# A convolution and attention mix: all of x loaded as rows, four buffers for VectorE's probabilities, GpSimd placed by VectorE, and 95 pairs of score tiles for VectorE

## The chip, the cores and the metric

The kernel runs on one core of a Trainium2 chip. The metric is device time in microseconds, the median of several runs; lower is better. A run takes a little longer than the span that its profile shows, from the first instruction to the last.

## The reference

x, k and v are 2048 tokens of 640 numbers in bfloat16. Two results are mixed by a gate of each token, `g = sigmoid(sum(x * gate_w))`.

```python
k_shift = sum over t of k_pad[:, t:t + S, :] * shift_k[:, ks - 1 - t]      # 4 taps along the tokens
kv = k_shift * v
y = causal convolution of kv with ssm_k along the tokens (by FFT) + kv * ssm_D
a = x * y
q = (x @ wq) as 32 heads of 20;  k = x @ wk;  v = x @ wv                  # one k and v for all heads
p = softmax((q . k) / sqrt(20));  b = (p . v) @ wo
out = g * a + (1 - g) * b
```

The convolution is done by matrices of cosines and sines (spectra of kv and ssm_k, a product, an inverse). The largest part is the softmax: 32 heads x 2048 x 2048 exponentials.

## The kernel before

**Attention.** The heads and token blocks make 32 groups `G` (four heads, 512 query tokens), each with 16 blocks `j` of 128 keys and four rows `r` (one for each head): 32 x 16 x 4 = 2048 score tiles of 128 x 512. A score is one matmul on 32 rows of TensorE (`score`, L1074), four rows side by side. ScalarE takes the exponential of three tiles in one call (`ETA`) and of two in the next (`ETB`), out of PSUM banks 0 to 4 (L1106). `PVmm` (L1146) multiplies the probabilities by v into bank 6, on 32 columns of TensorE for each row.

A table `DVE_J` gives for each group the key blocks of which two rows go to VectorE instead, a "pair": `DEXP` copies two scores out of banks 5 and 7 (L1135, `dW`) and evaluates a polynomial in three instructions of 128 x 1024 (L1138, L1139, L1141) into the one buffer `ETd`. Its PV, two matmuls with `vneg`, floats: it is put between the others when the pair is ready, and the last PV of the group waits for all pairs of the group.

**Beside it.** Between the scores TensorE does the shift of k (`kc`, L1325), the spectra (L1383) of five chunks of 128 channels, the inverse (L1449), the q projection of the next token block (L993), and the output projection (L1479); where it has nothing, it runs fillers on zeros (L1529). GpSimd multiplies the spectra (`mac`, L1416: `Pp`, then `AB`) and norms the attention's output (L1216). VectorE copies every result out of PSUM.

**Prologue.** Before the first exponential x must be there with its channels on the partitions (`xT`). Two of its four blocks of 512 tokens come by a DMA that transposes, issued by SP; the two others are loaded as rows (`xn`) and transposed on TensorE (L906), copied out by ScalarE (L631) and VectorE (L630). Then follow k, v and the gate's sum in one product (`kvn`, L942), the largest squared length of a key (`ksq`, `ksum`, `kmcol`, a broadcast on TensorE, `kmaxr`, `kroot`, `mcol`), which goes into k's row 21 as a bound for the softmax, the first q projection with its lengths (`sq`, `cr`, and a DMA of 8 KB into `qT`'s row 20, the "crow"), and `kT`, k for four rows. Eight sine and cosine tables of 128 x 513 are made by VectorE and ScalarE (L815 to L828). The two row blocks of x that came by the transposing DMA are loaded again as rows in the main part (`load_x`), for the gate and the product with x.

**What sets the order.** No order is written by hand. Every operation is recorded with what it reads and writes, a cost and a priority; `Scheduler` then places them one by one on five in-order engines, scores and exponentials first, the rest where the costs leave room, and emits each engine's list with semaphore waits. An instruction that waits holds up all that follow on its engine, in a list that was made by estimated costs.

## Time and profile before

| | before |
|---|---|
| median of 3 runs | 881.03 us (880.82 to 882.23) |
| the profiled execution's own time | 881.59 us |
| its span | 879.8 us |
| granted TensorE clock, mean | 0.999 |
| score tiles on VectorE, in pairs | 93 pairs |
| exponential calls on ScalarE | 745 |

The span is counted from the first instruction to the last; times of rows are from its start. A row of the view by time gives start, length, engine, line, operation, output and input, count, and in brackets how long the engine stood idle before it and what ended that. The chain of work that ended last is followed back from the last instruction, at each step to what released it. A group's row gives its busy time, the mean of one in ns, and the idle time ahead of it. In a table of stretches each engine's busy time stands with its count, and the last three columns are the granted clock, the DMA engines' busy share and GB/s.

### The profile page before, as it was taken

How to read it: one execution, taken by the hardware profiler on the slowest of the kernel's cores; microseconds unless marked ns; L12 is line 12 of the kernel's file. 1: busy time of each engine (PE TensorE's matmuls, PEld its weight loads, DVE VectorE, ACT ScalarE, POOL GpSimd, SP SyncE). 2: the span in 40 equal slices, each digit the busy share in tenths (PEclk: the TensorE clock that was granted, in tenths of full speed). 3: DMA queues.
4: the chain of work that ended last, by engine and by line, in shares of the span. 5: the costliest groups of instructions: out<-in, count | busy, mean ns of one | idle time of the engine just before them, and what ended most of it. 6: DMA issues, size and time to landing. Idle time of an engine off the chain costs nothing.

```text
span 879.8 us, 17975 instructions
## 1 busy us (share of the span) xinstructions
PE 852.8 (97%) x7783; PEld 345.5 (39%) x7804; DVE 683.1 (78%) x890; ACT 858.3 (98%) x770; POOL 434.3 (49%) x342
## 2 busy tenths in 40 slices
PE   7999999999999999999999999999999999999997
PEld 3335324442344334344334233444344444334333
DVE  6775887688878888887869886884878857878785
ACT  6999999999999999999999999999999999999995
POOL 2952005997064548734439823458764558510000
PEclk9999999999999999999999999999999999999999
DMA  8920310002000000100000111000000000302110
GB/s 160 222 80 20 57 30 21 13 9 43 20 20 20 14 9 19 45 19 20 13 17 11 44 38 39 20 10 11 20 20 19 14 13 2 102 22 74 51 36 32
DMA packets 55780, 31.98 MB, mean 36 GB/s; under 512 B 38547, under 2 KB 51732, under 8 KB 55700
## 3 DMA queue, kind: packets, MB, share of 16 engines
q1 hardware_dynamic: 53562, 29.79, 13.0%
q10 hardware_dynamic: 2138, 1.04, 0.5%
q8 instruction: 61, 1.00, 0.5%
q14 instruction: 19, 0.16, 0.1%
HBM read 17.85 MB, written 6.02 MB: 27 GB/s over the span
## 4 chain that ended last, share of the span: by engine, by line
ACT 84%; PE 12%; DMA 2%; DVE 1%; issue 0%; SPq 0%; DVEq 0%
ACT ETA L1106 51%; ACT ETB L1106 34%; PE ps L1074 4%; PE ps L1383 3%; PE ps L1146 2%; DMA xT<-in_A_q_dram 1%; PE ps L993 1%; PE ps L1529 1%; DMA qT<-cr 1%; PE ps L1325 0%; PE ps L1264 0%; DVE qT L1004 0%; PE ps L1015 0%; PE ps L1387 0%; DVE outsb L1288 0%; PE ps L1273 0%
## 5 line engine op out<-in xcount | busy, mean ns | idle before, releaser
L1106 ACT ACTIVATE ETA<-ps 128x1536 bf16<-128x1536 f32 (+1 forms) x373 | 582.7, 1562 | 1.5 <-PE ps L1074 1.1
L1106 ACT ACTIVATE ETB<-ps 128x1024 bf16<-128x1024 f32 x372 | 425.4, 1144 | 0.0
L1074 PE MATMUL ps<-qT,kT 32*128 32x512 bf16 x2048 | 302.1, 384 | 13.4 <-ACT ETA L1106 7.2
L1416 POOL TENSOR_TENSOR Pp<-X,K 128x512 f32<-128x512 bf16 x120 | 174.6, 1474 | 211.0 <-DVE K L1404 207.1
L1135 DVE TENSOR_SCALAR dW<-ps 128x512 f32<-128x512 f32 x186 | 127.5, 686 | 80.8 <-PE ps L1074 79.6
L1074 PEld LDWEIGHTS ps<-qT,kT 32*128 32x128 bf16 x2048 | 74.2, 91 | 243.6 <-ACT ETB L1106 118.5
L1146 PE MATMUL ps<-ETA,vaug 128*32 128x512 bf16 x1118 | 151.2, 385 | 0.0
L1146 PE MATMUL ps<-ETB,vaug 128*32 128x512 bf16 x744 | 148.8, 385 | 0.3 <-ACT ETA L1106 0.3
L1141 DVE SCALAR_TENSOR_TENSOR ETd<-dX,dW 128x1024 int16<-128x1024 f32 x93 | 126.1, 1356 | 13.4 <-PE ps L1146 13.3
L1138 DVE SCALAR_TENSOR_TENSOR dX<-dW 128x1024 f32<-128x1024 uint16 x93 | 129.8, 1395 | 1.1
L1139 DVE SCALAR_TENSOR_TENSOR dX<-dX,dW 128x1024 f32<-128x1024 f32 x93 | 125.4, 1348 | 0.4
L1416 POOL TENSOR_TENSOR AB<-Pp 128x256 bf16<-128x256 f32 x80 | 94.7, 1184 | 4.8
L1216 POOL TENSOR_TENSOR oTn<-acc,rbc 128x512 bf16<-128x512 f32 x24 | 38.1, 1588 | 90.6 <-DMA rbc<-scr_d 90.5
L1449 PE MATMUL ps<-AB,Tcos 128*128 128x256 bf16 x320 | 77.1, 275 | 0.0
L1529 PE MATMUL ps<-Tcos,zeros 128*32 128x512 bf16 x876 | 72.9, 385 | 0.0
L1416 POOL TENSOR_TENSOR Pp<-Pp 128x512 f32<-128x512 f32 x40 | 68.7, 1718 | 2.8
L1449 PE MATMUL ps<-AB,Tsin 128*128 128x256 bf16 x280 | 68.6, 275 | 0.0
L1216 POOL TENSOR_TENSOR oT<-acc,rbc 128x512 bf16<-128x512 f32 x7 | 12.1, 1732 | 94.1 <-DMA rbc<-scr_d 94.1
L1383 PE MATMUL ps<-ssm_kT,Tcos 128*128 128x256 bf16 x320 | 55.7, 276 | 0.0
L1383 PE MATMUL ps<-ssm_kT,Tsin 128*128 128x256 bf16 x320 | 51.1, 275 | 0.0
L1383 PE MATMUL ps<-kv,Tsin 128*128 128x256 bf16 x320 | 50.2, 274 | 0.0
L1383 PE MATMUL ps<-kv,Tcos 128*128 128x256 bf16 x320 | 49.0, 275 | 0.0
(140 smaller groups left out, 790.0 us busy)
## 6 DMA issues: line engine op xcount, KB each, us to landing
rbc<-scr_d SPq DMA_DIRECT2D x31, 256.0 KB
scr_o<-oTn SPq DMA_DIRECT2D x24, 128.0 KB, 1.9
kv<-in_A_v_dram SPq DMA_DIRECT2D x4, 640.0 KB
out_dram<-outsb SPq DMA_DIRECT2D x14, 160.0 KB, 2.8
xn<-in_A_q_dram SPq DMA_DIRECT2D x3, 640.0 KB
oTp<-scr_o SPq DMA_DIRECT2D x12, 160.0 KB, 2.9
wog<-in_B_wo_dram SPq DMA_DIRECT2D x4, 200.0 KB
wo<-in_B_wo_dram SPq DMA_DIRECT2D x4, 200.0 KB
```

The lines of the kernel that those rows point to most:

```text
L1074: return e.matmul(self.bank(bk), T["kT4"][32 * r:32 * r + 32, 128 * j:128 * j + 128], T[f"qT{G // 8 % 2}"][32 * r:32 * r + 32, G % 8, :], ...
L1106: op("act", lambda e: e.activation(et(n)[:, 0:w], self.ps[:, lo:lo + w], ACT.Exp, scale=SCALE), [("ps", base[n % 2] + k) for k in range(le ...
L1135: self.evac(gr, "dve", lambda e, bk, h=h: e.tensor_scalar(W[:, 512 * h:512 * h + 512], self.bank(bk), SCALE * LOG2E * 128.0, 128.0 * (127 ...
L1138: V(lambda e: e.scalar_tensor_tensor(X[:, :], w, DP, w, ALU.add, ALU.mult), [kW], ["dX"], c_ps(1024), **k)
L1139: V(lambda e: e.scalar_tensor_tensor(X[:, :], X[:, :], DQ, w, ALU.add, ALU.mult), [kW], ["dX"], c_ps(1024), **k)
L1141: V(lambda e: e.scalar_tensor_tensor(T["ETd"][:, :].bitcast(dt.int16), X[:, :], DA, W[:, :], ALU.mult, ALU.add), [kW, "dX"], ["ETd"], c_ps ...
L1146: return op("pe", lambda e: e.matmul(self.bank(6)[32 * r:32 * r + 32, :], T[va][:, j, :], src, start=(j == 0), stop=(j == NSC - 1), tile_p ...
L1216: self.pool(lambda e: e.tensor_tensor(out, T["acc"][:, :], T["rbc"][:, :], ALU.mult), ["acc", "rbc"], [key], c_pool(512), prio=p, port=Tru ...
L1383: self.mm(gr, lambda e, bk, lhs=lhs, rhs=rhs, comp=comp, n=n: e.matmul(self.bank(bk, 256, 256 * comp), lhs, rhs, start=(n == 0), stop=(n = ...
L1416: f = lambda e: e.tensor_tensor(out, a, b, alu)
L1449: self.mm(gr, lambda e, bk, lhs=lhs, fc=fc, comp=comp, h=h: e.matmul(self.bank(bk, 256, 256 * h), lhs, AB[:, fc, :, comp, :], start=(fc == ...
L1529: sch.filler = [[lambda e, r=r, st=st: e.matmul(self.bank(6)[32 * r:32 * r + 32, :], self.T["zeros"][:, 0:32], self.T["Tcos"][:, 0, 0:512] ...
```

## The change

It has six parts.

1. **x.** All four blocks of x are loaded as rows, first on SP's queue, and transposed on TensorE (80 transposes instead of 40). A channel of x goes to partition and chunk in another order (`dc:D:NDC`), and the rows of wk, wv, wq and gate_w with it, so that each partition reads one piece. `load_x` is gone.
2. **The rest of the prologue.** The first q projection is of one group instead of two; v's and the gate's copies out of the work tile go to GpSimd; `mcol` is a TENSOR_SCALAR; the first kT block is copied in two parts (128 and 384 columns), and the scores wait for the part that they read (`kkey`). The tables are made from column 128 c on; the part to its left is the transposed part of the other tables, made by TensorE after the first exponential. Many tiles share memory with others.
3. **VectorE's pairs.** `ETd` has four buffers (`NED`). Two floating pairs on different rows are put together (`join`), or a pair goes into a PV of two rows that leaves its rows free (`hole`).
4. **GpSimd.** `pool_may` lets the scheduler place a GpSimd instruction only while VectorE is in one that isn't marked `port`, or after it has waited long; and the instruction then waits for the VectorE instruction before that one.
5. **95 pairs** in another table `DVE_J`, in which a group has up to five.
6. `ssm_kT` has one buffer instead of two; the output's buffers lie over `qT0`.

```diff
+YOUNG = 4.0
+WAITN = 0.5
+HOLD = 0.1
+WAITP = 3.0
 PVB = 2
 NET = 3
+NED = 4
+NXK = 3
...
+        if e == "pool" and self.main_started and not self.pool_may(t):
+            return None
...
+    def pool_may(self, t):
+        d = self.order["dve"]
+        if not d or not HOLD:
+            return True
+        x = d[-1]
+        if not x.port and x.end > t + HOLD:
+            return True
+        w = [o.ready + (WAITP if o.name != "onorm" else WAITN) for o in self.cand["pool"] if o.ready <= t]
+        return bool(w) and t > min(w)
...
+                    self.join(f, t)
+                    return f
+        elif m.hole:
+            for f in self.floats:
+                if f.ready <= t and f.cols <= m.hole:
+                    self.floats.remove(f)
+                    self.float_left = list(f.tail)
+                    for x in f.tail:
+                        x.cost = 0.003
                     return f
...
+    def join(self, f, t):
+
+        for g in self.floats:
+            if g.ready <= t and not (g.cols & f.cols):
+                self.floats.remove(g)
+                self.float_left[-1].cost = 0.003
+                self.float_left += [g] + list(g.tail)
+                return
...
+        if e == "pool" and self.main_started and HOLD:
+            d = self.order["dve"]
+            if len(d) > 1 and d[-1].end > t and not d[-1].port:
+                op.deps.add(d[-2])
...
-DVE_J = [(6,), (), (2, 9, 14), (4, 10), (2, 9), (1, 2, 8, 12), (2, 7, 12), (2, 6, 10, 14), (3, 9), (1, 5, 12), (1, 7, 11), (2, 6, 10, 14), (2, 7, 12), (1, 4, 8, 12), (2, 5, 10), (1, 8), (2, 6, 10, 14), (3, 4, 13), (1, 4, 8, 12), (1, 9), (2, 10, 12), (3, 9), (2, 7, 12), (2, 5, 10, 14), (3, 6, 12), (1, 3, 9, 13), (12,), (3, 8, 13), (1, 6, 11), (3, 11, 12), (1, 5, 9, 13), (1, 5, 8, 12)]
+DVE_J = [(), (3, 11), (1, 6, 11), (2, 11), (2, 6, 10, 14), (3, 4, 9, 12), (3, 9), (1, 6, 11), (2, 8, 13), (1, 2, 7, 12), (2, 6, 10, 14), (3, 9), (1, 7, 10), (8,), (1, 4, 7, 10, 13), (3, 9), (1, 4, 8, 13), (2, 4, 8, 12), (1, 6, 11, 14), (6,), (3, 5, 8, 10), (1, 4, 8, 12), (8,), (1, 4, 7, 10, 13), (1, 4, 7, 10, 13), (1, 6, 11), (4,), (1, 4, 7, 10, 14), (2, 5, 8, 12, 14), (4, 11), (5,), (2, 9)]
...
-        for b in range(NB - 2):
-            o = T["xT"][:, :, 512 * b:512 * b + 512]
-            i = aps["A_q"][0][512 * b:512 * b + 512, :]
-            xl = self.g.add("sp", lambda e, o=o, i=i: e.dma_start_transpose(o, i), (), [("xT", b)], 0.1, kind="d",
-                            nbytes=655360, prio=-8 + b, lat=3.3)
-            xl.iss = 3.8
...
+        for b in range(NB):
+            xl = self.dma(T["xn"][:, 4 * b:4 * b + 4, :], x[:, 4 * b:4 * b + 4, :], writes=[("xn", b)], nbytes=655360,
+                          prio=-9 + b, lat=3.0)
...
+        wq = aps["B_wq"].rearrange("(p dc) n -> p dc n", dc=NDC)
+        self.dma(T["wqst"][:, :, 0:80], wq[:, :, 0:80], writes=[("wqst", 0)], eng="act", prio=-98.65,
+                 lat=4.5)
...
+            lo = 128 * c
+            n = W - lo
...
+            sins.append(self.op("act", lambda e, c=c, t=t, lo=lo: e.activation(
+                T["Tcs"][:, :, c, lo:W], t[:, :, lo:W], ACT.Sin, bias=T["pi_col"][:, :], scale=-2.0 * math.pi / L),
+                [("tprod", c), "pi_col"], [("Tsin", c), ("Tcos", c)], c_act(2 * n), **k))
...
+        for name in ("Tsin", "Tcos"):
+            gr = self.group("tabT", 12.0, banks=(7,))
+            for c in range(1, H):
+                for d in range(c):
+                    o = self.mm(gr, lambda e, bk, name=name, c=c, d=d: e.transpose(
+                        self.bank_bf(bk, 128, 64 * c * (c - 1) + 128 * d), T[name][:, d, 128 * c:128 * c + 128],
+                        T["ident"][:, :]), [(name, d), "ident"], 0.09)
...
-        for b, d0, nd in ((b, d0, nd) for b in (NB - 1, NB - 2) for d0, nd in ((0, 2), (2, 2), (4, 1))):
-            gr = self.group("xT", 0.5, banks=(0, 1, 2, 3, 4, 5, 7))
+        for b, d0, nd in ((b, d0, min(w, NDC - d0)) for b in range(NB) for w in (1 + (b < NB - 1),)
+                         for d0 in range(0, NDC, w)):
+            gr = self.group("xT", 0.5 + 0.1 * b, banks=(0, 1, 2, 3, 4, 5, 7))
...
-                        self.bank_bf(bk, 128, 512 * (dc - d0) + 128 * ci), T["xn"][:, i, 128 * dc:128 * dc + 128],
-                        T["ident"][:, :]), [("xn", b), "ident"], 0.09)
+                        self.bank_bf(bk, 128, 512 * (dc - d0) + 128 * ci), T["xn"][:, i, dc:D:NDC],
+                        T["ident"][:, :]), [("xn", b), "ident"], 0.068)
...
-    def load_x(self):
-        T = self.T
-        x = self.aps["A_q"][0].rearrange("(i p) d -> p i d", p=128)
-        for b in range(NB - 2):
-            self.dma(T["xn"][:, 4 * b:4 * b + 4, :], x[:, 4 * b:4 * b + 4, :], writes=[("xn", b)], nbytes=655360,
-                     prio=30 + b, name="ld_x", after=self.crow0)
+    def kkey(self, j):
+        return "kT4", j // 4, 128 if 0 < j < 4 else 0
...
-        self.dve(lambda e: e.scalar_tensor_tensor(T["mcol"][:, :], T["kroot"][:, :].bitcast(F32), T["m20"][:, 0:1],
-                                                  T["q21"][:, :], ALU.mult, ALU.add), ["kroot", "m20", "q21"],
-                 ["mcol"], 0.2, prio=-5000, name="kmax")
+        self.dve(lambda e: e.tensor_scalar(T["mcol"][:, :], T["kroot"][:, :].bitcast(F32), T["m20"][:, 0:1],
+                                           T["q21"][:, 0:1], ALU.mult, ALU.add), ["kroot", "m20", "q21"], ["mcol"], 0.2, prio=-5000, name="kmax")
```

Three places of the lists that the scheduler makes. First, ScalarE from its last tables on to the first exponential (`ksq` is the squares of the keys, ACT_TABLE_LOAD the change from sines to exponentials, `kT` the keys for the scores). Before:

```order
L828 ACTIVATE Tcos<-tcosp_54,pi_col 128x513
L825 ACTIVATE Tsin<-tprod_55,pi_col 128x513
L631 ACTIVATE xT<-ps 128x512
L948 ACTIVATE ksq<-ps 128x80 x2
L828 ACTIVATE Tcos<-tcosp_56,pi_col 128x513
L948 ACTIVATE ksq<-ps 128x80
L832 ACT_TABLE_LOAD
L832 ACTIVATE warm<-pi_col 1x1
L982 ACTIVATE kT<-ps,mcol 128x512 x2
L1106 ACTIVATE ETA<-ps 128x1536
```

Now:

```order
L864 ACTIVATE Tcs<-tprod_53,cols 128x2x257
L995 ACTIVATE ksq<-ps 128x80
L676 ACTIVATE xT<-ps 128x2x512
L676 ACTIVATE xT<-ps 128x512
L995 ACTIVATE ksq<-ps 128x80
L676 ACTIVATE xT<-ps 128x512 x3
L995 ACTIVATE ksq<-ps 128x80
L864 ACTIVATE Tcs<-tprod_54,cols 128x2x129
L995 ACTIVATE ksq<-ps 128x80
L868 ACT_TABLE_LOAD
L868 ACTIVATE warm<-cols 1x1
L1033 ACTIVATE kT<-ps,cols 128x128
```

More copies of xT stand among the squares, and one kT copy of 128 columns in place of two of 512 ahead of the exponential.

Second, TensorE around the first scores (L1129 scores, L979 the projections for kT, L1047 for q, L1202 PV). Now:

```order
L979 MATMUL ps<-xT,wk_85 128x512 x5
L1595 MATMUL ps<-ident,zeros 128x512
L1012 MATMUL ps<-ident,kmcol 128x128
L979 MATMUL ps<-xT,wk_85 128x512 x8
L1129 MATMUL ps<-qT,kT 128x512 x3
L979 MATMUL ps<-xT,wk_85 128x512 x7
L1129 MATMUL ps<-qT,kT 128x512 x5
L1047 MATMUL ps<-xT,wq_pad 128x512 x5
L1129 MATMUL ps<-qT,kT 128x512 x5
```

The first three scores stand alone, then seven projections, then the next five; before, five scores stood together behind twelve projections.

Third, TensorE where VectorE's probabilities come in (`ETd`), in the spectra of the first chunk. Before:

```order
L1074 MATMUL ps<-qT,kT 128x512 x3
L1146 MATMUL ps<-ETB,vaug 32x512
L1146 MATMUL ps<-ETA,vaug 32x512 x3
L1146 MATMUL ps<-ETB,vaug 32x512 x2
L1146 MATMUL ps<-ETA,vaug 32x512 x2
L1146 MATMUL ps<-ETd,vneg 32x512 x2
L1074 MATMUL ps<-qT,kT 128x512 x2
```

Now:

```order
L1129 MATMUL ps<-qT,kT 128x512 x3
L1202 MATMUL ps<-ETA,vaug 32x512
L1202 MATMUL ps<-ETd,vneg 32x512 x4
L1202 MATMUL ps<-ETA,vaug 32x512 x2
L1202 MATMUL ps<-ETB,vaug 32x512 x2
L1202 MATMUL ps<-ETA,vaug 32x512
L1129 MATMUL ps<-qT,kT 128x512 x3
```

Two pairs stand together, four matmuls, where each pair stood by itself with two; of the 95 pairs, 46 still do.

247 lines of the change are left out of this document (130 added, 117 removed).

## The prediction

> **What bounds the kernel now.** I read the page's busy shares and its chain of work that ended last, then the groups, then ScalarE's rows in order of time.
>
> ```profile
> span 879.8 us, 17975 instructions
> PE 852.8 (97%) x7783; PEld 345.5 (39%) x7804; DVE 683.1 (78%) x890; ACT 858.3 (98%) x770; POOL 434.3 (49%) x342
> ACT 84%; PE 12%; DMA 2%; DVE 1%; issue 0%; SPq 0%; DVEq 0%
> L1106 ACT ACTIVATE ETA<-ps 128x1536 bf16<-128x1536 f32 (+1 forms) x373 | 582.7, 1562 | 1.5 <-PE ps L1074 1.1
> L1106 ACT ACTIVATE ETB<-ps 128x1024 bf16<-128x1024 f32 x372 | 425.4, 1144 | 0.0
> ```
>
> ScalarE is busy 98% of the span and carries 84% of the chain; TensorE's 97% holds filler and modelled ends, and it carries 12%. So the exponentials set the time: 745 of them, three score tiles (ETA) and two (ETB) in turn. Their pace stands in the chain near the end:
>
> ```profile
> 839.16 0.92 ACT ETB L1106
> ...
> 868.54 0.92 ACT ETB L1106
> 869.46 0.93 ACT ETA L1106
> ...
> 876.65 0.79 DVE outsb L1288
> ```
>
> From 839.16 to 868.54 lie 13 pairs of calls: 2.26 us for five tiles. ScalarE's own rows show where that run begins and where it breaks:
>
> ```profile
> 20.57 0.24 ACT L948 ACTIVATE ksq<-ps 128x80 f32<-128x80 f32 x1 [0.35 <-PE ps L942]
> 20.82 1.28 ACT L832 ACT_TABLE_LOAD   x1
> 24.23 1.26 ACT L982 ACTIVATE kT<-ps,mcol 128x512 bf16<-128x512 f32 x2 [1.91 <-DVE mcol L973]
> 25.46 1.45 ACT L1106 ACTIVATE ETA<-ps 128x1536 bf16<-128x1536 f32 x1
> 49.33 1.10 ACT L1106 ACTIVATE ETB<-ps 128x1024 bf16<-128x1024 f32 x1
> 51.38 1.45 ACT L1106 ACTIVATE ETA<-ps 128x1536 bf16<-128x1536 f32 x1 [0.95 <-PE ps L1074]
> ```
>
> The span is then a sum of three: 25.46 of prologue, 844.93 of exponentials (25.46 to 869.46 + 0.93), 9.41 of tail (the last output projection, which the change leaves as it is). The middle holds 372 pairs and one call of two tiles, 372 x 2.26 + 0.93 = 841.65, and 3.28 of waits. Of these 1.13 is one gap: 51.38 - 49.33 is 2.05 for a call of 0.92. The other 2.15 is spread over the run (the gate's small exponential among it).
>
> **The change part by part.**
>
> *Two more pairs for VectorE.* The tables hold 93 and 95 pairs, so 190 instead of 186 of the 2048 tiles leave ScalarE: 1858 are left, 371 pairs of calls and one call of three, 371 x 2.26 + 1.34 (the 3-tile step, 2.26 - 0.92) = 839.80. That is **-1.85 us**, on the path in full.
>
> *The prologue.* The chain of the prologue begins with a transfer:
>
> ```profile
> 1.80 11.32 DMA xT<-in_A_q_dram
> 13.17 1.25 PE ps L993 x5
> ```
>
> The two DMA transposes of x land only at 13.1, and everything that leads to the first exponential stands behind them. The change loads all four blocks of x as rows, 4 x 655 KB, and with the early weights 2.77 MB. How fast rows come I bound by two windows:
>
> ```profile
> 2.00:15.00 13.00, 8.92 (x62) 4.41 (x64) 7.49 (x23) 6.76 (x9) 4.00 (x10) 1.00 1.18 220
> 43.50:48.50 5.00, 4.88 (x55) 2.04 (x46) 2.41 (x5) 5.00 (x6) 5.00 (x9) 1.00 1.05 374
> ```
>
> The prologue with its transposes moved 220 GB/s, a stretch of plain rows later 374 (last column). From 2.0 us on, the last block has moved at 9.4 by the one and 14.6 by the other; I take it nearer the first, since no transpose is left there. The block of x that is wanted first then comes early enough, and what comes next on the path are the TensorE transposes and the copies out of PSUM:
>
> ```profile
> 2.97 5.82 PE L1534 MATMUL ps<-ident,zeros 128*128 128x512 bf16 x15 [2.97 <-DVE ident L778]
> 8.62 1.06 PE L906 MATMUL ps<-ident,xn 128*128 128x128 bf16 x16
> 9.27 2.08 ACT L631 ACTIVATE xT<-ps 128x1024 bf16<-128x1024 bf16 x2 [1.51 <-PE ps L906]
> 15.28 0.72 ACT L825 ACTIVATE Tsin<-tprod,pi_col 128x513 bf16<-128x513 int32 x1
> 18.76 0.59 ACT L631 ACTIVATE xT<-ps 128x512 bf16<-128x512 bf16 x1
> ```
>
> TensorE stands in order behind its fillers: 15 from 2.97 to 8.79. The change has 12, about 1.1 us less, so the first copy can start at some 8.5 instead of 9.27 (8.2 at best). Forty more transposes cost 40 x 0.066 (1.06 for 16) = 2.6 us of TensorE, which now has nothing to do between 9.7 + 0.4 (four more of these) and 13.17. From its first copy to the last ksq the changed ScalarE has, by its order, 3 copies of 1024 at 1.04, 5 of 512 at 0.59, 4 ksq at 0.24, and tables of 770, 514 and 258 elements, which by the line through 0.24 (80 elements) and 0.72 (513) are 1.0, 0.72 and 0.44: together 9.2 us. 8.5 + 9.2 = 17.7; for waits among the three engines I add 0.5: 18.2, where it was 20.81. VectorE stands about as full; its copies go beside ScalarE's.
>
> From the last ksq to the first exponential the chain goes over VectorE:
>
> ```profile
> 20.84 0.24 DVE L956 TENSOR_REDUCE ksum<-ksq 128x4 f32<-128x80 f32 x1 [0.46 <-ACT ksq L948]
> 21.14 0.16 DVE L959 TENSOR_REDUCE kmcol<-ksum 128x1 bf16<-128x16 f32 x1
> 22.16 0.75 DVE L1004 TENSOR_SCALAR qT<-ps,qup 128x512 bf16<-128x512 f32 x1 [0.72 <-PE ps L993]
> 22.83 0.28 DVE L966 TENSOR_REDUCE kmaxr<-ps 128x1 f32<-128x128 f32 x1
> 23.14 0.15 DVE L970 TENSOR_SCALAR kroot<-kmaxr 128x1 int32<-128x1 int32 x1
> 23.33 0.86 DVE L973 SCALAR_TENSOR_TENSOR mcol<-kroot,m,q 128x1 f32<-128x1 f32 x1
> ```
>
> ```profile
> 24.97 0.60 PE L1074 MATMUL ps<-qT,kT 32*128 32x512 bf16 x5 [0.20 <-ACT kT L982]
> ```
>
> It took 4.89 us from the start of the last ksq (20.57 to 25.46). The change takes out of it the q projection and its copy between kmcol and kmaxr (some 0.9), writes mcol by the form that kroot has (0.15 for 0.86), and lets the first scores wait for a kT piece of 128 columns (about 0.3, between ksq's 0.24 and a 512's 0.68) instead of one of 512. That leaves 0.73 to kmcol's end, 0.5 for the broadcast on TensorE, 0.65 to mcol's end, 0.3 for kT and 0.49 (24.97 to 25.46) for the scores: 2.7, while the table load (1.28 and a short dummy call) fits beside it. First exponential at 18.2 - 0.24 + 2.7 = 20.7, I take 20.8: **-4.66 us**. Bounds: nothing waits and copies start at 8.2, 19.8; the last block lands at 14.6 + 1.8 (an 8 KB transfer of this trace, qT<-cr, took 1.84 to land), 1.5 us after ScalarE wants it, and the engines lose another 0.7: 23.0.
>
> *A new wait.* In the changed order seven projections for kT stand between the first and the second unit's scores. One comes every 0.22 us (5 in 1.25 at 13.17, the last of them 0.38 long), 1.5 us after the first scores, then 0.5 for the second scores, while the first exponential covers 1.34: **+0.65 us**.
>
> *The gap at 49.33 goes.* What was late there:
>
> ```profile
> 46.05 3.72 DMA qT<-cr
> ```
>
> 8 KB took 3.72 us, behind two blocks of x, 1.3 MB, that `load_x` fetches as rows in the main part. A score for VectorE's pair stood for it in TensorE's order, and the scores of ScalarE behind that. The x rows are not loaded there any more and the first pairs come later: **-1.13 us**. If the transfer waits behind the v rows instead, it costs the same again.
>
> *PV pairs that share slots, four buffers.* 24 times VectorE's pairs now go in groups of four or six matmuls, 25 slots of about 0.2 us less for TensorE. TensorE isn't on the path but for the 2.15 us of spread waits; I take nothing, and at best those.
>
> *Edits taken as nothing.* Half of the tables' lower parts are now made by 12 TensorE transposes and 6 VectorE copies after the first exponential, where TensorE runs fillers and ScalarE's pace covers them; uncovered they would cost some 12 x 0.07 + 6 x 0.4 = 3 us. ssm_kT has one buffer, so its next load follows the last use:
>
> ```profile
> DMA to landing us min/median/max: 3.4/3.4/3.4
> ```
>
> Between the last K of a chunk and the first of the next stand 22 score tiles or more in TensorE's new order, 22 / 5 x 2.26 = 9.9 us, which hides two loads of 3.4; without that cover each of four chunks would stand for up to 6.8.
>
> *GpSimd timed to VectorE.* Its instructions now wait for a VectorE instruction before the one they are to run beside. What they did to each other:
>
> ```profile
> L1008 DVE TENSOR_TENSOR sq<-qT x32: 348/416/1492, 15.6 to 527.5; 128x512 bf16<-128x512 bf16 x32
> ```
>
> ```profile
> L1416 POOL TENSOR_TENSOR Pp<-X,K 128x512 f32<-128x512 bf16 x120 | 174.6, 1474 | 211.0 <-DVE K L1404 207.1
> ```
>
> ```profile
> L1138 DVE SCALAR_TENSOR_TENSOR dX<-dW 128x1024 f32<-128x1024 uint16 x93 | 129.8, 1395 | 1.1
> L1135 DVE TENSOR_SCALAR dW<-ps 128x512 f32<-128x512 f32 x186 | 127.5, 686 | 80.8 <-PE ps L1074 79.6
> L1141 DVE SCALAR_TENSOR_TENSOR ETd<-dX,dW 128x1024 int16<-128x1024 f32 x93 | 126.1, 1356 | 13.4 <-PE ps L1146 13.3
> L1139 DVE SCALAR_TENSOR_TENSOR dX<-dX,dW 128x1024 f32<-128x1024 f32 x93 | 125.4, 1348 | 0.4
> ```
>
> The first row is of one instruction of VectorE, whose shortest, median and longest are 348, 416 and 1492 ns: some run beside GpSimd's and are stretched by up to a microsecond. GpSimd has 211 us of idle ahead of Pp alone, so holding it back costs nothing while that lasts. What VectorE gains reaches the path only where TensorE waits for it. Zero in the sum; the bound below is the 2.15. [...]
>
> **Sum.** -4.66 - 1.85 - 1.13 + 0.65 = -6.99 on the profiled execution: its span goes from 879.8 to 872.8. That execution took 881.59, 0.56 above the median 881.03 of the runs; the same difference on the median gives **874.0 us**.
>
> **The rivals.**
>
> *The spread waits go too.* VectorE is on time where it was stretched, so TensorE doesn't stand for it, and the prologue runs without its waits: 874.0 - 2.1 - 1.0 = 870.9. For it: the ranges above. Against: most of the waits can't be told from scores that simply stood behind one group too many. Chance 0.14.
>
> *The prologue gains half.* x lands late or the copies alternate badly: first exponential at 23.0, 876.2. For it: 220 GB/s was all that the prologue moved. Chance 0.14.
>
> *VectorE comes late with its pairs.* A pair costs it 1.395 + 1.348 + 1.356 + 2 x 0.686 = 5.47 us. The new table has five groups with five pairs (before: four at most): 27.4 us of VectorE in a group in which ScalarE needs 54 / 5 x 2.26 = 24.4. The last PV of a group waits for all its pairs, and scores stand behind it. If nothing is made up, five groups lose 3 us each: 889, slower. Against: neighbours of these groups have one pair or three, and four buffers let VectorE run ahead. It decides once more than 7 of the 15 us reach ScalarE. Chance 0.10.
>
> *The gain is mostly given back* in such waits without a loss: about 880.5. Chance 0.04.
>
> **How the numbers follow.** The forecast has 0.58. The range for 8 of 10 reaches from the first rival to the edge of the last, 870.8 to 880.0; the forecast's own is 872 to 876. Some 0.2% (1.8 us) can be told from no change here. Faster: 0.58 + 0.14 + 0.14 = 0.86; within 0.2%: 0.04; slower: 0.10.
>
> **What would show it.** First exponential near 20.8, and ScalarE without waits on PSUM copies of more than 0.5 before it; 743 exponentials at 2.26 a pair; 0.6 or so of idle after the first one; no gap like that at 49.33; sq nearer to its shortest, Pp below 1474. The prediction is wrong if the first exponential comes after 23, if ScalarE's rows in the five groups of five pairs show gaps behind TensorE that waits for ETd, or if the tail grows past 9.4.

## The result, and the profile after

| | before | changed |
|---|---|---|
| median of the runs beside each other | 881.63 us (4 runs, 880.82 to 883.49) | 882.29 us (4 runs, 879.47 to 883.05) |
| ratio to before, 95% interval | | 0.9999 [0.9971, 1.0027] |
| the profiled execution's own time | 881.59 us | 882.34 us |
| its span | 879.8 us | 880.5 us |
| first exponential starts | 25.46 | 25.55 |
| from there to the end of the last exponential | 844.58 | 845.13 |
| the same without waits, at 2.26 us a pair of calls | 841.64 | 839.80 |
| waits among the exponentials | 2.94 | 5.33 |
| from there to the end | 9.76 | 9.82 |

There is no change that can be measured. The last five rows are read from ScalarE's rows in order of time, for both kernels in the same way (the start of the last call, and 0.92 us for one of two tiles or 1.34 for one of three; the prediction's 844.93 took the last start from the chain, 0.34 later). So the prologue gained nothing, and the 1.85 us of exponentials that were saved went out again as 2.39 of waits.

The page of the changed kernel, its first, fourth and fifth part:

```profile
span 880.5 us, 18471 instructions
PE 859.4 (98%) x7956; PEld 351.3 (40%) x7956; DVE 715.9 (81%) x909; ACT 855.6 (97%) x765; POOL 378.0 (43%) x351
ACT 66%; PE 30%; DVE 3%; DMA 1%; issue 0%; ACTq 0%; DVEq 0%
L1161 ACT ACTIVATE ETA<-ps 128x1536 bf16<-128x1536 f32 x372 | 572.9, 1540 | 3.1 <-PE ps L1129 2.4
L1161 ACT ACTIVATE ETB<-ps 128x1024 bf16<-128x1024 f32 x371 | 415.0, 1119 | 0.5 <-PE ps L1129 0.5
```

372 and 371 calls are the 743 that were counted on. TensorE, which carried 12% of the chain before, now carries 30%: the pace is handed over to it in many more places.

**The prologue.** The chain of waits begins with a load of 1.2 KB, the gate's weights:

```profile
2.36 9.42 DMA gwr<-in_gate_w_dram
```

The rows in order of time say who stood for it (start, length, engine, line, operation, and in brackets the idle time before):

```profile
2.70 5.30 PE L1595 MATMUL ps<-ident,zeros 128*128 128x512 bf16 x12 [2.70 <-DVE ident L820]
11.35 0.52 POOL L938 COPY wq_pad<-wqst 128x400 bf16<-128x400 bf16 x1 [6.52 <-DMA wqst<-in_B_wq_dram]
11.81 0.18 DVE L935 COPY wkv<-gwr 128x5 bf16<-128x5 bf16 x1 [5.13 <-DMA gwr<-in_gate_w_dram]
12.56 0.94 ACT L864 ACTIVATE Tcs<-tprod,cols 128x770 bf16<-128x770 int32 x1 [2.96 <-DVE tprod L862]
13.51 0.86 PE L960 MATMUL ps<-ident,xn 128*128 128x128 bf16 x12 [3.15 <-DVE xT L675]
14.21 1.67 PE L1047 MATMUL ps<-xT,wq_pad 128*128 128x512 bf16 x5
25.55 1.45 ACT L1161 ACTIVATE ETA<-ps 128x1536 bf16<-128x1536 f32 x1 [0.92 <-PE ps L1129]
27.46 1.02 ACT L1161 ACTIVATE ETB<-ps 128x1024 bf16<-128x1024 f32 x1 [0.46 <-PE ps L1129]
```

The load is issued at 2.36, fourth on ScalarE's queue, while the four blocks of x go out on SP's, and it has landed only at 11.8. A copy of 5 columns of it (L935) stands in VectorE's list; VectorE is idle for 5.13 us in front of it, and behind it stand the angles of the tables (ScalarE is idle for 2.96) and the first copies of xT (TensorE is idle for 3.15). The first 80 columns of the q weights, issued third, land at 11.35 and hold GpSimd in the same way. x itself came fast, as the table of stretches shows (last column GB/s, the third from the end the granted TensorE clock):

```profile
4.00:6.00 2.00, 2.00 (x6) 0.71 (x5) 0.64 (x3) 1.99 (x3) 0.73 (x3) 1.00 1.07 383
8.00:10.00 2.00, 1.47 (x25) 1.34 (x24) 0.00 (x0) 1.02 (x1) 0.00 (x0) 1.00 1.11 306
11.00:12.00 1.00, 0.00 (x0) 0.00 (x0) 0.19 (x2) 0.00 (x0) 0.65 (x2) 1.00 0.06 21
15.00:18.00 3.00, 3.00 (x39) 2.48 (x36) 1.99 (x7) 1.50 (x4) 0.39 (x2) 0.50 0.34 119
```

383 and 306 GB/s, and from 11 to 12 us only 21: both small loads land when x is in. And from 15 to 18 the clock is 0.50, after the idle time of TensorE; the five projections from 14.21 on took 1.67.

**Among the exponentials.** The gap of 1.13 at 49.33 is gone, and 0.57 has come after the first call (27.46). The rest of the waits grew from 1.81 to 4.76. They are a sum over all calls, and a pair without a gap takes a little less than 2.26, so the gaps themselves sum to more: without the two named, those of 0.10 and over sum to 5.81 before (31 of them) and to 7.43 now (38). Some 1.6 of the growth of 2.95 is in them, and the rest is spread over the calls in smaller amounts. The largest single one:

```profile
177.21 0.38 PE L1129 MATMUL ps<-qT,kT 32*128 32x512 bf16 x1 [0.66 <-DVE dW L1191]
177.53 1.05 PE L1590 MATMUL ps<-Tcs,zeros 128*32 128x512 bf16 x16
178.51 0.39 PE L1129 MATMUL ps<-qT,kT 32*128 32x512 bf16 x3
179.00 1.45 ACT L1161 ACTIVATE ETA<-ps 128x1536 bf16<-128x1536 f32 x1 [0.65 <-PE ps L1129]
```

A score for VectorE's pair stands 0.66 for VectorE's copy out of its bank, 16 fillers come behind it, and only then the three scores that ScalarE wants. The others are smaller, 0.1 to 0.5: in most the three scores of an ETA stand behind one group of spectra or PV too many. Fillers are among what TensorE ran just ahead (from 1 us before the start of the call in front of the gap) in 7 of the 38, the largest among them, with 2.15 of the 7.43; in the other 31 TensorE ran work of the kernel alone.

**VectorE and GpSimd** (groups with busy time and mean ns; the tile's row with shortest, median, longest):

```profile
L1475 POOL TENSOR_TENSOR Pp<-X,K 128x512 f32<-128x512 bf16 x120 | 159.9, 1349 | 152.9 <-DVE ETd L1197 36.3
L1475 POOL TENSOR_TENSOR AB<-Pp 128x256 bf16<-128x256 f32 x80 | 65.1, 813 | 87.6 <-DVE dX L1194 32.8
L1194 DVE SCALAR_TENSOR_TENSOR dX<-dW 128x1024 f32<-128x1024 uint16 x95 | 135.3, 1424 | 0.9
L1195 DVE SCALAR_TENSOR_TENSOR dX<-dX,dW 128x1024 f32<-128x1024 f32 x95 | 135.4, 1425 | 0.3
L1197 DVE SCALAR_TENSOR_TENSOR ETd<-dX,dW 128x1024 int16<-128x1024 f32 x95 | 132.7, 1397 | 5.5 <-PE ps L1202 5.1
L1062 DVE TENSOR_TENSOR sq<-qT x32: 409/417/1169, 16.8 to 531.2; 128x512 bf16<-128x512 bf16 x32
```

The timing rule made GpSimd faster (Pp 1474 to 1349) and not VectorE: its three long instructions for a pair are longer by 29, 77 and 41 ns, and sq has the median that it had, though its longest fell from 1492 to 1169.

### The profile page after: what moved, and what is told of

It is laid out like the page before. It is cut to its first block, busy times and chain, and to the rows that moved or that the text cites. A ratio compares the mean times of both kernels' runs of the same rounds, so it can differ in the third digit from the quotient of the medians.

```text
span 880.5 us, 18471 instructions
## 1 busy us (share of the span) xinstructions
PE 859.4 (98%) x7956; PEld 351.3 (40%) x7956; DVE 715.9 (81%) x909; ACT 855.6 (97%) x765; POOL 378.0 (43%) x351
## 4 chain that ended last, share of the span: by engine, by line
ACT 66%; PE 30%; DVE 3%; DMA 1%; issue 0%; ACTq 0%; DVEq 0%
ACT ETA L1161 39%; ACT ETB L1161 26%; PE ps L1129 9%; PE ps L1442 7%; PE ps L1202 5%; PE ps L1508 3%; PE ps L1538 2%; PE ps L1590 1%; DMA gwr<-in_gate_w_dram 1%; PE ps L1301 1%; DVE ETd L1197 1%; DVE dX L1195 1%; PE ps L979 1%; DVE dW L1191 0%; PE ps L1446 0%; DVE dX L1194 0%
## 5 line engine op out<-in xcount | busy, mean ns | idle before, releaser
L1161 ACT ACTIVATE ETA<-ps 128x1536 bf16<-128x1536 f32 x372 | 572.9, 1540 | 3.1 <-PE ps L1129 2.4
L1129 PE MATMUL ps<-qT,kT 32*128 32x512 bf16 x2048 | 297.8, 384 | 8.5 <-ACT ETA L1161 4.3
L1475 POOL TENSOR_TENSOR Pp<-X,K 128x512 f32<-128x512 bf16 x120 | 159.9, 1349 | 152.9 <-DVE ETd L1197 36.3
L1129 PEld LDWEIGHTS ps<-qT,kT 32*128 32x128 bf16 x2048 | 73.4, 91 | 233.9 <-ACT ETB L1161 110.7
L1202 PE MATMUL ps<-ETA,vaug 128*32 128x512 bf16 x1116 | 153.1, 385 | 0.0
L1202 PE MATMUL ps<-ETB,vaug 128*32 128x512 bf16 x742 | 147.3, 385 | 0.0
L1475 POOL TENSOR_TENSOR AB<-Pp 128x256 bf16<-128x256 f32 x80 | 65.1, 813 | 87.6 <-DVE dX L1194 32.8
L1442 PE MATMUL ps<-ssm_kT,Tcs 128*128 128x256 bf16 x600 | 95.5, 275 | 0.5 <-DVE dW L1191 0.4
L1442 PE MATMUL ps<-kv,Tcs 128*128 128x256 bf16 x600 | 89.2, 275 | 0.0
L1508 PE MATMUL ps<-AB,Tcs 128*128 128x256 bf16 x600 | 88.8, 274 | 0.0
L1590 PE MATMUL ps<-Tcs,zeros 128*32 128x512 bf16 x980 | 81.0, 385 | 0.7 <-DVE acc L1264 0.6
L1276 POOL TENSOR_TENSOR oTn<-acc,rbc 128x512 bf16<-128x512 f32 x24 | 40.8, 1698 | 72.9 <-DMA rbc<-scr_d 30.6
L1442 PEld LDWEIGHTS ps<-ssm_kT,Tcs 128*128 128x128 bf16 x600 | 48.3, 97 | 44.5 <-issue 31.5
L1442 PEld LDWEIGHTS ps<-kv,Tcs 128*128 128x128 bf16 x600 | 49.5, 98 | 37.5 <-issue 30.2
L1508 PEld LDWEIGHTS ps<-AB,Tcs 128*128 128x128 bf16 x600 | 51.3, 98 | 31.8 <-issue 26.7
L1047 PE MATMUL ps<-xT,wq_pad 128*128 128x512 bf16 x160 | 46.0, 386 | 0.0
```

Source lines behind the costliest of these rows:

```text
L1047: o = self.mm(gr, lambda e, bk, gi=gi, dc=dc: e.matmul(self.bank(bk), T["wq_pad"][:, dc, 128 * gi:128 * gi + 128], T["xT"][:, dc, 512 * I: ...
L1129: return e.matmul(self.bank(bk), T["kT4"][32 * r:32 * r + 32, 128 * j:128 * j + 128], T[f"qT{G // 8 % 2}"][32 * r:32 * r + 32, G % 8, :], ...
L1161: op("act", lambda e: e.activation(et(n)[:, 0:w], self.ps[:, lo:lo + w], ACT.Exp, scale=SCALE), [("ps", base[n % 2] + k) for k in range(le ...
L1202: return op("pe", lambda e: e.matmul(self.bank(6)[32 * r:32 * r + 32, :], T[va][:, j, :], src, start=(j == 0), stop=(j == NSC - 1), tile_p ...
L1442: self.mm(gr, lambda e, bk, lhs=lhs, rhs=rhs, comp=comp, n=n: e.matmul(self.bank(bk, 256, 256 * comp), lhs, rhs, start=(n == 0), stop=(n = ...
L1475: f = lambda e: e.tensor_tensor(out, a, b, alu)
```

## The experiments

The scheduler lays out the whole program again when one operation is added or one constant changes. So most experiments leave its layout as it is and edit the finished lists, between its run and the emission of the instructions; four let it lay out anew, and are marked so. Each ran beside the kernel before on the same chip (its medians were 881.28 for the f runs, 880.57 for the g runs and 882.69 for the h runs). All numbers but the medians and ratios are from the profiled executions, one for each kernel, read as in the table above.

| run | median us | ratio to before | first exponential | exponentials | waits | to the end | span |
|---|---|---|---|---|---|---|---|
| changed kernel | 882.29 | 0.9999 [0.9971, 1.0027] | 25.55 | 845.13 | 5.33 | 9.82 | 880.5 |
| f1 gate's weights first | 878.35 | 0.9954 [0.9937, 0.9971] | 23.27 | 845.14 | 5.34 | 9.89 | 878.3 |
| f2 q's weights first too | 876.60 | 0.9933 [0.9917, 0.9950] | 19.64 | 845.01 | 5.21 | 9.85 | 874.5 |
| f4 fillers in the idle time | 880.44 | 0.9977 [0.9964, 0.9991] | 24.00 | 845.18 | 5.38 | 9.82 | 879.0 |
| f3 no GpSimd waits | 883.44 | 1.0018 [1.0003, 1.0033] | 23.69 | 847.44 | 7.64 | 9.87 | 881.0 |
| g0 one pair moved, new layout | 890.21 | 1.0111 [1.0093, 1.0128] | 21.17 | 844.21 | 4.41 | 23.02 | 888.4 |
| g1 GpSimd rule off, new layout | 891.14 | 1.0120 [1.0105, 1.0135] | 20.45 | 848.59 | 8.79 | 20.36 | 889.4 |
| g2 the old 93 pairs, new layout | 889.10 | 1.0093 [1.0074, 1.0112] | 20.62 | 853.50 | 11.86 | 14.38 | 888.5 |
| g3 no shared slots, new layout | 897.20 | 1.0187 [1.0172, 1.0202] | 20.00 | 842.52 | 2.72 | 32.68 | 895.2 |
| h1 scores earlier at 6 places | 878.03 | 0.9947 [0.9927, 0.9968] | 20.59 | 845.29 | 5.49 | 9.82 | 875.7 |
| h2 scores earlier at 39 places | 880.30 | 0.9979 [0.9966, 0.9992] | 20.50 | 848.45 | 8.65 | 9.85 | 878.8 |
| h4 as h2, fewer fillers | 878.38 | 0.9952 [0.9938, 0.9967] | 19.81 | 846.69 | 6.89 | 9.90 | 876.4 |

### The prologue: f1, f2 and f4

f1 puts the gate's load in front on ScalarE's queue:

```diff
         sch.run()
+        gw = self.g.writer["gwr"]
+        for l in (sch.order["act"], sch.linear):
+            l.remove(gw)
+            l.insert(0, gw)
```

> The changed kernel with every list as it is, but the gate's weights (gwr, 1.2 KB) are issued first on ScalarE's queue instead of fourth. Theory A, behind x: a small load that is issued after the rows of x lands only when x is in. Then gwr, issued ahead of x, lands by 4.5 instead of 11.8, VectorE does not stand 5.1 us for it, the xT copies and the tables come as early as their transposes allow, TensorE's idle of 3.15 before its last 12 of the first 40 transposes falls below 1; the q weights still land at some 11.3 and the q projection then starts at 12 to 12.5; first exponential 21.5 to 23.5 (25.55 in the changed kernel), span 876.5 to 878.5. Rival B, a load of 10 bytes a partition is slow by itself: gwr takes some 9 us wherever it stands, lands at 10 and the first exponential comes at 24 or later.

```profile
7.82 0.17 DVE L935 COPY wkv<-gwr 128x5 bf16<-128x5 bf16 x1
11.31 0.52 POOL L938 COPY wq_pad<-wqst 128x400 bf16<-128x400 bf16 x1 [5.17 <-DMA wqst<-in_B_wq_dram]
11.88 1.73 PE L1047 MATMUL ps<-xT,wq_pad 128*128 128x512 bf16 x5 [1.53 <-POOL wq_pad L938]
```

Theory A, in nearly all that it forecast. VectorE reads the gate's weights at 7.82 without a wait, the first 40 transposes are through 4.0 us earlier, and the next late load shows: the q weights land at 11.31 still, GpSimd copies them, TensorE starts the q projection at 11.88. Ahead of x the load of ten bytes a partition took 7.1 us at most, from its issue at 0.74 to that read, instead of 9.42. The first exponential gained 2.28. That is with the low clock once more: it was 0.50 from 12.5 to 15.9 in this execution, and the five projections took 1.73. The other five executions of f1 have a mean clock of 0.999 or 1.00 and spans 1.6 to 2.0 shorter. By its letter theory A is too strong: the weights of k and v, issued at 1.20 and 1.68 with x under way, are used at 5.38 and 7.30, long before x is in (nothing moves from 11 to 12, after 215 GB/s from 10 to 11).

f2 puts the q weights in front of x as well:

```diff
+        w0 = self.g.writer[("wqst", 0)]
+        sch.order["act"].remove(w0)
+        sch.order["sp"].insert(0, w0)
+        sch.linear.remove(w0)
+        sch.linear.insert(0, w0)
+        w0.eng = "sp"
```

> As the one before, and the first 80 columns of the q weights are issued first on SP's queue, ahead of x, instead of on ScalarE's behind two others; the rest as it is. Theory A: they land by 5 instead of 11.3, nothing but x and the engines is left in the prologue, first exponential 20.3 to 21.5 (x some 0.5 later), no stretch below 0.9 of the granted TensorE clock after 14 us, span 874.5 to 876.5. Rival C, the q projection is not on the chain once VectorE is free: first exponential within 0.4 of the one before. Rival B as there: 24 or later.

```profile
2.71 4.22 PE L1595 MATMUL ps<-ident,zeros 128*128 128x512 bf16 x12 [2.71 <-DVE ident L820]
4.66 0.52 POOL L938 COPY wq_pad<-wqst 128x400 bf16<-128x400 bf16 x1
7.41 1.02 ACT L676 ACTIVATE xT<-ps 128x1024 bf16<-128x1024 bf16 x1 [2.49 <-PE ps L960]
9.70 1.24 PE L1047 MATMUL ps<-xT,wq_pad 128*128 128x512 bf16 x5
16.31 0.24 ACT L995 ACTIVATE ksq<-ps 128x80 f32<-128x80 f32 x1 [0.27 <-PE ps L987]
```

The same 100 KB that took from 1.70 to 11.35 behind x are copied at 4.66 when they go ahead of it, and the projection runs at 9.70 without a wait. The first exponential comes at 19.64, 5.9 us earlier than in the changed kernel and earlier than theory A had it; rivals B and C fall. The exponentials took 845.01 against 845.13: the time won ahead of them stayed won.

Part of the 5.9 is the luck of f2's execution. TensorE's first 12 fillers, the same in all versions, take 4.22 us here and took 5.30 in the changed kernel, and the transposes come behind them. h1 and h2 below have the same lists up to the first exponential; their fillers take 5.07 and 5.09, and their first exponentials come at 20.59 and 20.50. Over the eight versions with these loads first it comes between 19.64 and 21.17, and the fillers take between 4.22 and 5.30, the shortest and the longest in the same two versions.

The trace shows how slowly a small load on a second queue comes through beside a large one. In the changed kernel the 640 pieces of the q weights, of 160 bytes each, start between 5.87 and 10.74, among pieces of x of 1280 bytes, which start until 11.44; in f2, ahead of x, the same 640 start between 2.19 and 3.56. The gate's 128 pieces of 10 bytes, issued behind those of q on the same queue, start between 8.75 and 11.27. What x alone and what the q weights ahead of it cost the gate's load isn't separated, since f1 moves it ahead of both.

f4 leaves the loads late and gives TensorE 12 fillers where it stood for 3.15 us:

```diff
+        at = sch.order["pe"][39]
+        i = sch.linear.index(at)
+        for n in range(12):
+            f = Op("pe", sch.filler0, c_mm(512), "c", "fill", 0.0)
+            f.deps.update(sch.fill0_deps)
+            sch.order["pe"].insert(40 + n, f)
+            sch.linear.insert(i + 1 + n, f)
```

> The changed kernel with its loads as they are; 12 more fillers of TensorE stand ahead of the last 12 of the first 40 transposes, where TensorE was idle for 3.15 us and after which its granted clock was 0.50 from 15 to 18. Theory D, the idle brings the low clock and the low clock costs time: the clock stays at 1.0 through 18, five q projections take 1.25 instead of 1.67 and 20 of the kv products 0.66 instead of 0.91, and the first exponential comes 0.8 to 1.7 earlier, 23.9 to 24.8. Theory A alone, all of the lost time is VectorE that stands for the gate: clock 1.0 but first exponential 25.3 to 25.6.

```profile
15.00:18.00 3.00, 3.00 (x68) 2.54 (x67) 2.92 (x9) 2.54 (x4) 0.39 (x2) 1.00 0.28 96
```

Theory D: the clock stays at 1.00, five projections take 1.24, and the first exponential comes 1.55 earlier (24.00) with the loads as late as before. All twelve executions of f4 have a mean clock of 0.999 or 1.00; of the changed kernel's four one has. So of the 5.9 us some 1.5 were the low clock that the idle time brought, and the rest was the standing itself, with the pace of the first fillers in it.

### GpSimd timed to VectorE: f3

```diff
+                op.held = None if d[-2] in op.deps else d[-2]; op.deps.add(d[-2])
...
         sch.run()
+        for o in sch.linear:
+            o.deps.discard(getattr(o, "held", None))
```

> The changed kernel with every engine's list as it is, but without the waits that were added so that a GpSimd instruction starts with the VectorE instruction it was put beside. Theory E, these waits cost VectorE: GpSimd beside it from the start of long VectorE instructions stretches those (dX 1424, ETd 1397 ns where before had 1395 and 1356), and TensorE's waits for VectorE's copies follow; without them dX is back at 1395 to 1405, the waits spread over the exponentials fall from 5.33 to some 3.3, the span by 2. Rival F, the waits come from the order (where pairs, fillers and scores stand) and not from GpSimd's moment: the gaps at 177, 364 and 145 stay, the spread waits stay within 0.7 of 5.33. By the first rival of the prediction (the hold frees VectorE) it is slower by 1 to 3 us. GpSimd's Pp goes from 1349 towards 1474 ns in each case.

```profile
L1475 POOL TENSOR_TENSOR Pp<-X,K 128x512 f32<-128x512 bf16 x120 | 178.1, 1504 | 166.5 <-DVE K L1463 120.4 <-DVE AB L1491 45.5
L1475 POOL TENSOR_TENSOR AB<-Pp 128x256 bf16<-128x256 f32 x80 | 97.7, 1222 | 5.2
267.75 1.87 DVE L1194 SCALAR_TENSOR_TENSOR dX<-dW 128x1024 f32<-128x1024 uint16 x1
270.67 0.39 PE L1129 MATMUL ps<-qT,kT 32*128 32x512 bf16 x1 [0.64 <-DVE K L1463]
```

Neither theory. Without the waits GpSimd is slower (AB 813 to 1222, Pp 1349 to 1504), VectorE's three instructions of a pair are faster together (4.13 us instead of 4.25), and yet the exponentials wait 2.3 us longer: gaps of 0.71 and 0.68 come at 270 and 493, where TensorE stands for VectorE's copies K and dW, made late by single instructions of VectorE of some 2 us beside GpSimd's. The gaps at 177 and 364 that rival F wanted to see again are gone, and the one at 145 stays. So the waits are worth 2.3 us to this layout as a sum and cost VectorE 0.1 a pair; they may have their part in single gaps, but taken together the growth of the spread waits isn't theirs. (The first exponential is at 23.69 with the same loads, in an execution in which TensorE's clock stayed at 1.00.)

### New layouts: g0 to g3

All four are made from f2, so their prologues are the quick one. g0 moves one pair of the second group by one key block, g1 turns the rule for GpSimd off, g2 takes the table of 93 pairs, g3 takes out `join` and `hole`:

```diff
-DVE_J = [(), (3, 11), (1, 6, 11),
+DVE_J = [(), (4, 11), (1, 6, 11),
...
-HOLD = 0.1
+HOLD = 0.0
...
-                    self.join(f, t)
+                    pass
...
-        elif m.hole:
+        elif False:
```

> Base is the kernel with the gate's and q's weights first (f2), whose exponentials run from 19.64 for 845.0 us, 5.2 of it waits beyond 371 x 2.26 + 1.34; the kernel before had 845.0 with 3.3 of waits for two calls more. Here one pair of the second group stands at key block 4 instead of 3, and the planner lays out everything anew. It shows what a new layout does by itself. If waits are a matter of how the layout falls, the stream differs by more than 0.7 from 845.0 in either direction; if they come with the rules and the number of pairs, it stays within 0.4.

> Base f2 (stream 845.0). The rule that times GpSimd to VectorE is off, and the planner lays out everything anew (in f3 the waits alone were taken out under the old layout, and the stream grew by 2.3). Theory, the rule is worth something also against a layout made without it: stream 846 to 847.5, Pp and AB longer by 100 ns and more. Rival, f3 lost only since its layout was made for the waits: stream 844.6 to 845.4. If the rule costs, below 844.5.

> Base f2 (743 calls, stream 845.0). The table of 93 pairs of the kernel before in the changed kernel: 745 calls, 841.65 without waits. Theory P, the two pairs more brought as many waits as they saved: waits at 3.0 to 3.8, stream 844.7 to 845.4. Rival R, the pairs pay in full and the new rules cost the waits: waits at 4.8 to 5.6, stream 846.4 to 847.2, span 876 or more.

> Base f2 (stream 845.0). Each pair's two PV matmuls go by themselves again, with no slot shared, and the planner lays out everything anew; 95 pairs and four buffers stay. Theory S, four or six PV matmuls in one place stand before scores and make the new waits: stream shorter by 0.8 to 2. Rival T, shared slots free TensorE where scores are short of time: stream longer by 0.8 to 3. Within 0.5: the sharing does nothing for the waits.

Only g0 falls near what was put: its exponentials are 0.80 shorter than f2's, where 0.7 was the line for a matter of layout. g1 is longer than any of its three cases, with one gap of 4.26 at 790, though Pp and AB grew as its theory had it (1532 and 1258 ns). g2 lies far outside both of its cases, and g3 is 2.49 shorter, theory S's way and more than it had. Together they answer another question. One pair moved by one key block, a change with no meaning of its own, costs 13.9 us of span, and almost all of it behind the last exponential: 23.02 instead of 9.85. Without shared slots the exponentials are the fastest of all, 842.52 with 2.72 of waits, and the end comes 22.8 later. The chain of g3 shows what is there:

```profile
863.58 3.50 PE ps L1508 x31
...
867.86 5.35 PE ps L1538 x35
873.21 2.45 PE ps L1301 x18
875.66 6.00 PE ps L1538 x40
881.66 4.10 PE ps L1301 x30
```

The end of the inverse transform of the last chunk (L1508), most of two token blocks' output projections (L1538) and a part of the last block's (L1301) are left over when ScalarE is done. In the changed kernel the spectra end at 770 us, the inverse at 836 and these projections at 859; in the kernel before at 745, 807 and 848; in g0 at 791, 854 and 872; in g3 at 807, 867 and 882. The work beside the scores is a second chain, which ends 11 us ahead of the last exponential in the changed kernel, 22 ahead in the kernel before, and behind it in g0 and g3. It isn't TensorE's time alone that makes it late: the inverse of the last chunk waits for GpSimd's products, the last of which ends at 790 in the changed kernel and at 812 in g0, and from the end of the spectra to there TensorE's fillers are half of the time:

```profile
770.00:790.00 20.00, 10.09 (x136) 1.00 0.05 15
791.00:812.00 21.00, 10.83 (x156) 1.00 0.04 14
```

The first line is of the changed kernel's fillers alone (stretch, length, their busy time and count, clock, DMA share, GB/s), the second of g0's. Where the chain loses its time ahead of that, and why one pair moved is enough, isn't shown. The old table in the new kernel (g2) fits no better than one pair moved. Its gaps come early, some of them while the clock was 0.50 (from 24.8 to 31.6), and 3.4 us at 49.54 alone, where the next scores stand for the 8 KB of `qT<-cr`:

```profile
50.63 2.69 DMA qT<-cr
```

So whether two pairs more pay for themselves can't be read from a new layout, whose own scatter (842.52 to 853.50, and 14.38 to 32.68 behind) is many times their 1.85.

### Scores earlier: h1, h2 and h4

In f2's layout the three scores are moved ahead of as many of the operations before them as the gap is long, at places that the trace of f2 names; h4 also leaves out four fillers behind 21 of the places, 84 in all, and spreads the seven kT projections after the first scores. The edit of h1:

```diff
+        for n, c in [(106, 0.53), (134, 2.0), (152, 0.25), (298, 0.57), (452, 0.31), (522, 0.28)]:
+            blk = sorted((d for d in ex[n].deps if d.name == "qk"), key=pe.index)
+            dep = set().union(*(b.deps for b in blk))
+            s = pe.index(blk[0])
+            j = s
+            while pe[j - 1].name != "qk" and pe[j - 1] not in dep and (c > 0 or pe[j - 1].cost < 0.01):
+                j -= 1
+                c -= pe[j].cost
+            del pe[s:s + len(blk)]
+            pe[j:j] = blk
```

> f2 with every list as it is, but at six places on TensorE the three scores of the next exponential stand ahead of what they stood behind: at four of them PV matmuls of VectorE's pairs, at two of them work that stood for VectorE's copy dW. In f2 these six gaps sum to 2.5 us of 5.2. Theory V, a gap is one group too many ahead of the scores and nothing else, and the growth of the spread waits against the kernel before sits at VectorE's pairs: the six gaps fall below 0.1 each and nothing comes in their place, stream 842.3 to 843.0 instead of 845.0, span 872 to 872.8. Rival K, TensorE is full and the time comes back as gaps behind the work that was passed: stream 844 to 845.

> As h1, at all 39 places of f2 with a gap of 0.10 or more after the first (7.8 us together). Theory V: stream 837.5 to 839.5, waits below zero against 2.26 a pair, since the pair without any gap takes some 2.25; span 867 to 869. Rival K, TensorE is full: more than half comes back elsewhere, stream 841 to 844, or as a longer tail (over 11.2 from the last exponential's start).

> As h2; after each of the 39 places four fillers of TensorE are left out, so that the passed work is not late; and the seven kT projections between the first and the second unit's scores are spread behind the following scores, which takes the 0.57 after the first exponential. Theory V: stream 0.5 shorter than h2's. Rival K with fillers as the cause: stream 1 to 3 shorter than h2's. Clock stays at 1.0 in both.

Rival K, and more so than it was put. At six places nothing is won (845.29 for 845.01), at 39 the exponentials take 3.4 us longer, and with fewer fillers still 1.7 longer; h4 is 1.76 shorter than h2, as rival K had it with the fillers as a cause. One place of the 39, first in f2, where a gap of 0.14 stood behind five projections:

```profile
43.28 1.25 PE L1047 MATMUL ps<-xT,wq_pad 128*128 128x512 bf16 x5
44.46 0.39 PE L1129 MATMUL ps<-qT,kT 32*128 32x512 bf16 x3
44.95 1.55 ACT L1161 ACTIVATE ETA<-ps 128x1536 bf16<-128x1536 f32 x1
```

and the same in h2, some 0.9 later on its clock:

```profile
45.17 0.39 PE L1129 MATMUL ps<-qT,kT 32*128 32x512 bf16 x3 [0.20 <-ACT ETA L1161]
45.50 0.61 PE L1047 MATMUL ps<-xT,wq_pad 128*128 128x512 bf16 x2
...
47.26 0.59 PE L1047 MATMUL ps<-xT,wq_pad 128*128 128x512 bf16 x2
47.79 0.39 PE L1129 MATMUL ps<-qT,kT 32*128 32x512 bf16 x3
...
48.28 1.45 ACT L1161 ACTIVATE ETA<-ps 128x1536 bf16<-128x1536 f32 x1
```

The scores now come early, TensorE stands 0.20 for ScalarE to free the banks, and the projections that were passed stand ahead of the next three scores: the next ETA starts at 48.28, 0.35 late. There are no fillers in this stretch, from 43 to 48 us: TensorE has no time to spare in it, so a gap there isn't a matter of who comes first. In h4 the wait after the first exponential was only cut up, into 0.40, 0.19 and 0.35. What stays open is how much of the growth from 1.81 to 4.76 belongs to the two pairs and how much to the layout; every layout tried gave another number, and the pairs weren't tried alone in one layout.

f2 is the fastest version found: 876.6 us, ratio to before 0.9933 [0.9917, 0.9950]; h1, at 0.9947 [0.9927, 0.9968], can't be told from it.

## Why the prediction was wrong

The forecast was 874.0, from a span 6.99 shorter; the span became 0.7 longer. The difference of 7.69 is 4.75 in the prologue, 2.88 among the exponentials and 0.06 behind them.

- **Two more pairs, -1.85.** Right as a term: 743 calls, 839.80 without waits.
- **The prologue, -4.66: measured +0.09.** The step that failed is "The block of x that is wanted first then comes early enough, and what comes next on the path are the TensorE transposes and the copies out of PSUM". x did come early enough, all of it by some 11 us (between the bounds of 9.4 and 14.6); but what came next on the path was the landing of the gate's 1.2 KB at 11.8, which wasn't priced at all, nor what stands behind a waiting copy in VectorE's list (5.13 of idle there, 3.15 on TensorE, and the low clock). The prediction asked what TensorE's list stands behind, the fillers, and didn't ask it of VectorE's. Its own sign of being wrong, a first exponential after 23, came. Of the 4.75 some 1.5 to 1.9 is the low clock: with the same late loads and a clock of 1.00 the first exponential came at 24.00 in f4 and at 23.69 in f3. With the late loads removed (f2) the rest of the step holds: 19.64, and 20.59 and 20.50 with the slower first fillers of h1 and h2, where 20.8 was put and 19.8 was the best bound. Its parts in f2: the first copy at 7.41 (put at 8.5; 8.57 in the changed kernel, whose fillers took 5.30), the last ksq at 16.31 (put at 17.96), and 3.33 from there to the first exponential (put at 2.7: eight projections stand ahead of the first scores, so the exponential comes 0.92 after the end of the kT copy instead of 0.49).
- **A new wait, +0.65.** Right, 0.57.
- **The gap at 49.33, -1.13.** It is gone, as put, but not shown to be gone for the reason given. In g2, which doesn't load the rows of x there either, the same transfer took 2.69 us with 6 GB/s moving in all, and the exponentials stood 3.4 for it. What stands behind the transfer in the layout decides, at least as much as what it waits behind.
- **Shared slots and the spread waits, nothing.** The step that failed: "TensorE isn't on the path but for the 2.15 us of spread waits; I take nothing, and at best those". The bound was put on one side only. These waits became 4.76. Why they grew stays open. What the runs show: in 31 of the 38 gaps of 0.10 and over TensorE ran work of the kernel and no filler, and scores moved ahead there (h1, h2) won nothing, so in these stretches it has no time to spare; g0 and g3 show that the work beside the scores comes at the end where it isn't done in time, at 13 to 23 us. Over the whole run TensorE isn't full, and there the prediction's "filler and modelled ends" has a point: its fillers were busy for 72.9 us before and for 81.0 now.

```profile
L1529 PE MATMUL ps<-Tcos,zeros 128*32 128x512 bf16 x876 | 72.9, 385 | 0.0
L1590 PE MATMUL ps<-Tcs,zeros 128*32 128x512 bf16 x980 | 81.0, 385 | 0.7 <-DVE acc L1264 0.6
```

- **Edits taken as nothing.** None of them shows as a gap: the table transposes at 25.4 in f2 lie under the exponentials, and no stand at ssm_kT's load is among the gaps.
- **GpSimd timed to VectorE, nothing.** As a sum it couldn't be told; in the trace GpSimd gained and VectorE lost a little, the opposite of what the rival "the spread waits go too" needed. f3 gives the rule 2.3 us in this layout.
- **The tail.** 9.76 to 9.82, as put; g0 to g3 (14.38 to 32.68) show that it hangs on the layout and is no property of the change.
- **The rivals.** "The gain is mostly given back" came nearest with 880.5 and had the smallest chance; it was thought of as waits for VectorE, and only part of it was that. "The prologue gains half" had the right place and the wrong mechanism: not x but what is queued behind it. VectorE was not late in the groups of five pairs: no gap over 0.4 lies there.

## What to carry to other kernels

When a large load is put first, list every small load that is issued after it, when each is first read, and what stands behind that reader on its engine; issue the small ones ahead of the large one, which here was worth 5.9 us between the profiled executions, some 1.5 of it by the clock, for two moved instructions. When an engine's busy share is near that of the bound, look at what it holds in the stretches where the bound waits, work or filler, before taking it as free or as full; and take for any saving there the scatter that a new layout brings by itself. To test a part of a kernel whose order is made by a planner, edit the finished lists; a new layout tests the layout.

## What the runs showed of the hardware

- A load of 1.2 KB on ScalarE's queue, behind 100 KB in pieces of 160 bytes, took 9.42 us while 2.6 MB were moving on SP's; in front of them (f1), issued at 0.74, its reader found it ready at 7.82 without a wait.
- TensorE's clock fell to 0.50 for some 3.4 us (from 14.9 to 18.3) after an idle time of 3.15, but stayed at 1.00 after 2.85 in f3; in f1 it fell after an idle time of only 1.53 that had been preceded by shorter ones (2.65 us busy of the 5 from 8 to 13), and in g2 after idle times of at most 0.95 (1.07 us busy of the 2 from 22 to 24), for 6.8 us. Of the changed kernel's four runs three show a mean clock of 0.995 to 0.997, and the one at 1.00 is 2.8 us shorter. With the same list the clock falls in one execution and not in another; what sets the moment isn't shown.
- TensorE's first 12 fillers, the same list, took from 4.22 to 5.30 us in the profiled executions of the twelve versions with the new prologue.
- The rule that starts GpSimd with a VectorE instruction sped GpSimd's AB from 1222 ns (f3, without its waits) to 813 and slowed VectorE's pair by 0.12 us (4.13 in f3, 4.25).
